# Linear attention by halves of 64 tokens in the last two of four sequences

## The chip, the cores and the metric

The program runs on one core of a Trainium2 chip. Its engines are TensorE (PE in the profile, with PEld for its weight loads), VectorE (DVE), ScalarE (ACT), GpSimd (POOL) and SyncE (SP, which issues most DMAs). The metric is the device time of one execution in microseconds, 890.63 us as the median of three runs (887.6 to 891.57).

## The reference

Four sequences of 576 tokens go through causal attention without a softmax (8 heads of 64, with a decay per head), and then through two feed-forward layers of 512 to 2048 to 512:

```python
ret = scores * Dmat          # scores = q k^T / sqrt(64); Dmat = gamma**(i-j) for i >= j, else 0
x = np.matmul(ret, v)        # per head; heads side by side make 2304 tokens x 512
h = x @ w_in;  g = np.where(h > 0, h, np.exp(np.minimum(h, 0)) - 1);  x = g @ w_out
h = np.maximum(x @ w_in2, 0);  out = (h * h) @ w_out2
```

## The kernel before

The decay is taken into q and k beforehand (`scale_chunk`, L261: one multiplication each on DVE, or on POOL for the first block). Attention then runs by chunks of up to 128 tokens, each in three pieces (`attn_pieces`, L271):

- `transposes` (L288): q and k to heads-by-tokens on PE, two heads to a group of 128 partitions, and copied out by ACT into `qT` and `kT`.
- `scores` (L300): per head K·Qᵀ, masked by DVE (L309) into `P0` (even heads) and `P1` (odd heads; `P1` takes the place of `kT`).
- `values` (L315): what earlier tokens give is read from the state `st` (L321), what the chunk itself gives is P·V (L325), both into one PSUM bank, which is split into a high and a low float32r part (`split`, L157: ACT, then DVE). Then KᵀV of the chunk (L335) is added to `st` by DVE (L341).

Attention is in plain float32: each such matmul of the program leaves two records in the trace, each with its own weight load. `st` is block-diagonal: of each 128x128 block, two heads' 64x64 squares are filled. PSUM for attention is a pool of two banks (`ps_a`, L142) through which all its tiles rotate; q, k and v have two buffers each (`n_p`, L137).

The tokens lie in five blocks (`BLOCKS`, L24; 512, 512, 256, 512, 512). The first layer is done unit by unit (`up`, L353, twelve matmuls of 128x128 weights; `down`, L374, twelve more, two units later), and the pieces of attention for the next block stand between ACT's and DVE's part of a unit (`mid`, L798), by `SPREAD` (L41). A chunk's loads are issued after the chunk two before it is done (`load_next`, L716). The first two sequences' chunks lie in the first block, the second and the first half of the third; the chunks of the last two sequences are done during the units of the second, third and fourth block. A scheduler then sets the order on each engine by its own estimate of times, and each engine works in that order; PE's matmuls of the layers and of attention stand between one another.

Of the kernel before, what the change touches and what calls it, by code (L numbers as in the profile page):

```python
# [9 lines left out]
F32 = mybir.dt.float32  # L10
# [4 lines left out]
ALU = mybir.AluOpType  # L15

B, H, S, D = 4, 8, 576, 64
NT, DM, DFF = B * S, H * D, 2048
P = 128
NP = H // 2  # L20
KC = DM // P
NF = DFF // P
TB = 512
BLOCKS = [(0, 512), (512, 512), (1024, 256), (1280, 512), (1792, 512)]  # L24
NB = len(BLOCKS)
LAG = 2
WARM = 3

AHEAD = 2
# [32 lines left out]
CW = COLS // NCH  # L62
NU = COLS // P
COL0 = [t // 2 for t, _ in BLOCKS]
# [8 lines left out]
def tokens(half, u):  # L73

    blk = max(b for b in range(NB) if COL0[b] <= u * P)
    t, n = BLOCKS[blk]
    return t + half * n // 2 + u * P - COL0[blk]

# [1 line left out]

MOST = float(np.array([0x7F7FF000 >> 3], np.uint32).view(np.float32)[0])

C_ID, C_MASK, C_S = 0, 128, 256


def chunks_of_blocks():
# [3 lines left out]
    for t, n in BLOCKS:  # L90
        end, cs = t + n, []
        while t < end:
            b, s = divmod(t, S)
            n = min(P, S - s, end - t)
            cs.append((b, s, n))
# [9 lines left out]
def scale_cols(s):  # L105
    c = C_S + 2 * H * STARTS.index(s)
    return c, c + H


def constants():  # L110


    c = np.zeros((P, C_ALL), np.float64)
    i = np.arange(P)
    gamma = 1.0 - 2.0 ** (-5.0 - np.arange(H))
    c[:, C_ID:C_ID + P] = np.eye(P)
    c[:, C_MASK:C_MASK + P] = i[:, None] <= i[None, :]
    for s in STARTS:
        e = (s + i - S // 2)[:, None].astype(np.float64)
        cq, ck = scale_cols(s)  # L120
        c[:, cq:cq + H] = gamma[None, :] ** e / np.sqrt(D)
        c[:, ck:ck + H] = gamma[None, :] ** -e
    return c.astype(np.float32)
# [3 lines left out]
def tile_kernel(ctx: ExitStack, tc, q, k, v, w_in1, w_out1, w_in2, w_out2, cst, out):  # L127
    nc = tc.nc
    pool = lambda name, bufs, **kw: ctx.enter_context(tc.tile_pool(name=name, bufs=bufs, **kw))
    const = pool("const", 1)  # L130
# [19 lines left out]

    wo2s = dram.tile([7 * HF, P, 2, DM // 2], F32, tag="wo2s", name="wo2s")
    cs = const.tile([P, C_ALL], F32, name="cs")
    st = const.tile([P, NP, P], F32, name="st")
    ident, mask = cs[:, C_ID:C_ID + P], cs[:, C_MASK:C_MASK + P]


    def split(pair_hi, pair_lo, src, eng=nc.vector):  # L157

        nc.scalar.copy(pair_hi, src)  # L159
        eng.tensor_tensor(out=pair_lo, in0=src, in1=pair_hi.bitcast(F32), op=ALU.subtract)  # L160
# [56 lines left out]
    def fetch_w(u, spare=None):  # L217
        a = a_p.tile([P, NP, P], F32, tag=spare, name="f") if spare else f_p.tile([P, DM], F32, tag="f", name="f")
        if spare:
            a = a.rearrange("s a b -> s (a b)")  # L220
        nc.sync.dma_start(out=a, in_=w2s[u[1] * NF + u[2]])
        f32s[u] = a
# [13 lines left out]
    nat, spare = {}, {}  # L236
    x_t = {}
# [23 lines left out]
    def scale_chunk(ch):  # L261
# [4 lines left out]
        for t, c in zip((qn, kn), scale_cols(ch[1])):  # L266
            eng.tensor_tensor(
                out=t[:n], in0=t[:n], in1=cs[:n, c:c + H].unsqueeze(2).to_broadcast([n, H, D]), op=ALU.mult
            )

    def attn_pieces(ch, blk):  # L271
        b, s, n = ch
        o = b * S + s - BLOCKS[blk][0]
        live = {}

        def psum(name, w=P):
            if ch in aside[::2]:
                return ps_acc.tile([P, 512], F32, tag="acc", name=name)[:, :NP * w].rearrange("s (p i) -> s p i", p=NP)
            return ps_a.tile([P, NP, w], F32, tag="a", name=name)

        def sbuf(name):
            if ch not in aside:

                return a_p.tile([P, NP, P], F32, tag="kT" if name == "P1" else name, name=name)

            return spare[ch][("P1", "k", "v", "qT", "kT", "P0").index(name)].rearrange("s (p i) -> s p i", p=NP)

        def transposes():  # L288
            qn, kn, _ = nat[ch]
            for t, nm in ((qn, "qT"), (kn, "kT")):  # L290
                ps = psum("ps_t")
                for p in range(NP):
                    nc.tensor.transpose(
                        ps[:, p, :n], t[:n, 2 * p:2 * p + 2, :].rearrange("s h d -> s (h d)"), ident[:n, :n]
                    )
                tt = sbuf(nm)
                live[nm] = tt
                nc.scalar.copy(tt[:, :, :n], ps[:, :, :n])

        def scores():  # L300
            qT, kT = live["qT"], live["kT"]
            ps = [psum("ps_s") for e in range(2)]
            for p in range(NP):
                for e in range(2):
                    r = slice(e * D, (e + 1) * D)
                    nc.tensor.matmul(ps[e][:n, p, :n], kT[r, p, :n], qT[r, p, :n], start=True, stop=True)  # L306
            for e in range(2):
                pt = sbuf(f"P{e}")
                nc.vector.tensor_tensor(  # L309
                    out=pt[:n, :, :n], in0=ps[e][:n, :, :n],  # L310
                    in1=mask[:n, :n].unsqueeze(1).to_broadcast([n, NP, n]), op=ALU.mult,
                )
                live[e] = pt

        def values():  # L315
            qT = live["qT"]
            _, kn, vn = nat[ch]
            ps = psum("ps_o")

            for p in range(NP if s else 0):  # L320
                i = nc.tensor.matmul(ps[:, p, :n], st[:, p, :], qT[:, p, :n], start=p == 0, stop=True, skip_group_check=True)  # L321
                tc.stamp_issue_order_token(i.ins, f"state{b}_{s}")
            for p in range(NP):
                for e in range(2):
                    nc.tensor.matmul(  # L325
                        ps[e * D:(e + 1) * D, p, :n], vn[:n, 2 * p + e, :], live[e][:n, p, :n],
                        start=not s, stop=True, skip_group_check=True,
                    )
            x = x_t[blk]
            split(x[:, :, 0, o:o + n], x[:, :, 1, o:o + n], ps[:, :, :n])  # L330
            if s + n < S:
                pu = psum("ps_u", D)
                for p in range(NP):
                    for e in range(2):
                        nc.tensor.matmul(  # L335
                            pu[e * D:(e + 1) * D, p, :], kn[:n, 2 * p + e, :], vn[:n, 2 * p + e, :], start=True, stop=True
                        )
                for e in range(2):
                    r = slice(e * D, (e + 1) * D)
                    if s:  # L340
                        nc.vector.tensor_tensor(out=st[r, :, r], in0=pu[r], in1=st[r, :, r], op=ALU.add)  # L341
                    else:
                        nc.vector.tensor_copy(st[r, :, r], pu[r])
            del nat[ch]

        return [transposes, scores, values]


# [356 lines left out]
    w2 = [(1, 0, f + h * HF) for f in range(HF) for h in range(2)] + [(1, 1, f + h * HF) for f in range(HF) for h in range(2)]  # L705

    nc.sync.dma_start(out=cs, in_=cst)
    nc.vector.memset(st, 0.0)

    warm = ps_h.tile([P, 512], F32, tag="h", name="warm")  # L710
    for _ in range(WARM):
        nc.tensor.matmul(warm, st[:, 0], st.rearrange("p a b -> p (a b)"), start=True, stop=True)
    at = dict(load=0, scale=0, next=0, raw=0, f32=0, split=0, raw2=0, f322=0, park=0, fetch=0, split2=0)
    todo = []

# [10 lines left out]
    def attn_step():  # L726
        if not todo and at["next"] < len(chunks):
            ch, blk = chunks[at["next"]]
            if blk not in x_t:
                new_x(blk)  # L730
            todo.extend(attn_pieces(ch, blk))
            at["next"] += 1
        if todo:
            todo.pop(0)()
            if len(todo) == 1:
                scale_next()
            if not todo:
                load_next()
# [23 lines left out]

    new_x(0)
    first = [attn_pieces(ch, 0) for ch in blocks[0]]
    load_next()
    load_next()
# [30 lines left out]
    for i, (blk, f) in enumerate(ORDER1):  # L797
# [30 lines left out]
        pend.append((blk, f))  # L828
        if len(pend) > LAG:
            down(*pend.pop(0))  # L830
# [76 lines left out]
```

## Time and profile before

| | |
|---|---|
| median of three runs | 890.63 us |
| profiled execution, span of it | 890.2 us, 888.4 us |
| busy: PE, PEld, DVE, ACT | 858.9, 773.1, 685.8, 491.9 us |
| granted TensorE clock over the span | 0.99 |

The profile is of one execution. Times in rows are microseconds from the start of the span. A PE record's end is modelled, and records of one engine overlap, so what a matmul costs is read from the distance between starts. Attention of the last two sequences lies at about 230 to 410 us, the first layer ends near 520 us.

### The profile page before, as it was taken

How to read it: one execution, taken by the hardware profiler on the slowest of the kernel's cores; microseconds unless marked ns; L12 is line 12 of the kernel's file. 1: busy time of each engine (PE TensorE's matmuls, PEld its weight loads, DVE VectorE, ACT ScalarE, POOL GpSimd, SP SyncE). 2: the span in 40 equal slices, each digit the busy share in tenths (PEclk: the TensorE clock that was granted, in tenths of full speed). 3: DMA queues.
4: the chain of work that ended last, by engine and by line, in shares of the span. 5: the costliest groups of instructions: out<-in, count | busy, mean ns of one | idle time of the engine just before them, and what ended most of it. 6: DMA issues, size and time to landing. Idle time of an engine off the chain costs nothing.

```text
span 888.4 us, 14958 instructions
## 1 busy us (share of the span) xinstructions
PE 858.9 (97%) x5630; PEld 773.1 (87%) x5630; DVE 685.8 (77%) x1391; ACT 491.9 (55%) x961; POOL 8.6 (1%) x12
## 2 busy tenths in 40 slices
PE   7798999999998999999999999999999989999998
PEld 5676888888888988888888899999989989999997
DVE  4998888885667867766779867889874769898984
ACT  3674778673464666556767754555543434444441
POOL 3000000000000000000000000000000000000000
PEclk9999899999999999999999999999999999999999
DMA  9945306383528656534362044599997993544331
GB/s 223 269 117 160 87 33 190 119 213 96 142 60 233 173 156 184 171 107 146 129 230 89 24 126 154 161 325 349 344 324 242 402 346 132 157 141 154 120 131 37
DMA packets 157608, 155.33 MB, mean 175 GB/s; under 512 B 62816, under 2 KB 121312, under 8 KB 157536
## 3 DMA queue, kind: packets, MB, share of 16 engines
q1 hardware_dynamic: 150208, 139.69, 52.0%
q10 hardware_dynamic: 7328, 14.68, 4.6%
q8 instruction: 44, 0.72, 0.4%
q14 instruction: 28, 0.23, 0.1%
HBM read 98.77 MB, written 55.57 MB: 174 GB/s over the span
## 4 chain that ended last, share of the span: by engine, by line
PE 83%; DVE 6%; DMA 5%; issue 2%; ACT 2%; SPq 1%; ACTq 0%; DVEq 0%
PE m L675 18%; PE A L492 10%; PE acc L163 7%; PE acc L164 7%; PE h L163 7%; PE acc L165 7%; PE h L164 7%; PE h L165 7%; PE D L492 5%; PE B L492 2%; PE ps_o L325 2%; PE ps_o L321 1%; PE ps_s L306 1%; DMA q<-in_q_dram 1%; DMA g<-g2s 1%
## 5 line engine op out<-in xcount | busy, mean ns | idle before, releaser
L675 PE MATMUL m<-wo,S 128*128 128x256 f32 x1512 | 184.0, 285 | 3.6 <-ACT S L159 3.6
L675 PEld LDWEIGHTS m<-wo,S 128*128 128x128 f32 x1512 | 183.3, 193 | 4.1 <-ACT S L159 4.0
L159 ACT CAST S<-g 128x512 fp32r<-128x512 f32 (+1 forms) x144 | 75.0, 567 | 95.0 <-DVE g L659 45.9
L163 PE MATMUL h<-x,w 128*128 128x512 f32 (+1 forms) x320 | 120.4, 378 | 2.2 <-DVE t L370 1.3
L164 PE MATMUL h<-x,w 128*128 128x512 f32 (+1 forms) x320 | 118.9, 372 | 0.0
L165 PE MATMUL h<-x,w 128*128 128x512 f32 (+1 forms) x320 | 118.9, 371 | 0.0
L164 PE MATMUL acc<-g,w 128*128 128x512 f32 (+1 forms) x320 | 118.5, 371 | 0.0
L165 PE MATMUL acc<-g,w 128*128 128x512 f32 (+1 forms) x320 | 117.5, 370 | 0.0
L492 PE MATMUL A<-T,pair 128*128 128x384 f32 x576 | 114.2, 339 | 1.6 <-DVE go L519 0.8
L163 PE MATMUL acc<-g,w 128*128 128x512 f32 (+1 forms) x320 | 111.4, 375 | 2.3 <-DVE x L402 1.3
L492 PEld LDWEIGHTS A<-T,pair 128*128 128x128 f32 x576 | 102.0, 190 | 3.4 <-DVE go L519 1.6
L160 DVE TENSOR_TENSOR S<-g,S 128x512 fp32r<-128x512 f32 (+1 forms) x144 | 85.9, 623 | 23.2 <-ACT S L159 21.7
L365 ACT ACTIVATE t<-h 128x512 f32<-128x512 f32 (+1 forms) x80 | 44.5, 556 | 80.5 <-PE h L165 76.9
L369 DVE SCALAR_TENSOR_TENSOR t<-e,t 128x512 f32<-128x512 f32 (+1 forms) x80 | 50.9, 636 | 46.7 <-ACT t L367 46.5
L163 PEld LDWEIGHTS h<-x,w 128*128 128x128 f32 x320 | 60.7, 190 | 14.1 <-DVE t L370 1.8
L159 ACT CAST g<-t 128x512 fp32r<-128x512 f32 (+1 forms) x80 | 46.4, 580 | 46.5 <-DVE t L370 44.7
L163 PEld LDWEIGHTS acc<-g,w 128*128 128x128 f32 x320 | 59.4, 188 | 13.4 <-DVE x L402 1.6
L165 PEld LDWEIGHTS h<-x,w 128*128 128x128 f32 x320 | 60.8, 190 | 10.7 <-DVE w L160 0.2
L164 PEld LDWEIGHTS h<-x,w 128*128 128x128 f32 x320 | 60.9, 190 | 10.2
L164 PEld LDWEIGHTS acc<-g,w 128*128 128x128 f32 x320 | 60.3, 188 | 10.2
L165 PEld LDWEIGHTS acc<-g,w 128*128 128x128 f32 x320 | 60.2, 188 | 10.1
L492 PE MATMUL D<-T,pair 128*128 128x384 f32 x288 | 58.5, 336 | 1.9 <-ACT pair L159 0.6
(88 smaller groups left out, 1282.4 us busy)
## 6 DMA issues: line engine op xcount, KB each, us to landing
g2s<-go SPq DMA_DIRECT2D x48, 384.0 KB, 4.5
g<-g2s SPq DMA_DIRECT2D x36, 512.0 KB, 3.9
raw<-in_moe_w_in_dram SPq DMA_DIRECT2D x32, 512.0 KB, 5.8
raw<-in_moe_w_out_dram SPq DMA_DIRECT2D x32, 512.0 KB, 4.8
wo2s<-wo SPq DMA_DIRECT2D x56, 256.0 KB, 4.2
wo<-wo2s ACTq DMA_DIRECT2D x9, 1536.0 KB, 14.7
w2s<-f SPq DMA_DIRECT2D x32, 256.0 KB, 2.3
f<-w2s SPq DMA_DIRECT2D x32, 256.0 KB, 4.0
```

The lines of the kernel that those rows point to most:

```text
L159: nc.scalar.copy(pair_hi, src)
L160: eng.tensor_tensor(out=pair_lo, in0=src, in1=pair_hi.bitcast(F32), op=ALU.subtract)
L163: nc.tensor.matmul(ps, l_hi, r_hi, start=first, stop=False)
L164: nc.tensor.matmul(ps, l_hi, r_lo, start=False, stop=False)
L165: nc.tensor.matmul(ps, l_lo, r_hi, start=False, stop=last)
L306: nc.tensor.matmul(ps[e][:n, p, :n], kT[r, p, :n], qT[r, p, :n], start=True, stop=True)
L321: i = nc.tensor.matmul(ps[:, p, :n], st[:, p, :], qT[:, p, :n], start=p == 0, stop=True, skip_group_check=True)
L325: nc.tensor.matmul(ps[e * D:(e + 1) * D, p, :n], vn[:n, 2 * p + e, :], live[e][:n, p, :n], start=not s, stop=True, skip_group_check=True,)
L365: nc.scalar.activation(t, h, AF.Relu, scale=-1.0)
L369: nc.vector.scalar_tensor_tensor(out=t, in0=e, scalar=1.0, in1=t, op0=ALU.add, op1=ALU.mult)
L492: ins = nc.tensor.matmul(ps, w[:, l, o:o + P], t[:, r, j], start=first and i + j == 0, stop=i + j == 3, skip_group_check=True)
L675: ins = nc.tensor.matmul(m(u, k), l[:, x], w[:, y], start=first and k in (1, 6, 4, 5), stop=j == HF - 1 and i == 2, skip_group_check=True,)
```

## The change

The first two sequences keep their code (now `scores_whole` and `values_whole`). `P0` no longer has a buffer: for chunks that don't lie in spare room it takes the place of the chunk's own q. The last two sequences go by halves of 64 tokens within a chunk. Scores are made only for the two squares on the diagonal (64 keys by 64 queries per head); the lower left square is left to the state, which now advances by 64 tokens and has two buffers, `sts`, used in turn. A half's KᵀV is made in the scores piece, in the same two PSUM banks as the scores, and added to the state from one buffer into the other; the second half's is first copied by ACT to where q was, and added at the end of `values`. Both masked halves of P lie in the place of `kT`. The values of a half are read from its own state (128 rows by 64 columns of weights, 64 tokens) and from P. The constants get a 64-column mask, and both states are cleared at the start.

```diff
-C_ID, C_MASK, C_S = 0, 128, 256
+C_ID, C_MASK, C_HALF, C_S = 0, P, 2 * P, 2 * P + HC
...
             if ch not in aside:
-
+                if name == "P0":
+                    return nat[ch][0].rearrange("s h d -> s (h d)").rearrange("s (p i) -> s p i", p=NP)
...
+        def add_state(to, st, u):
+            for (out_, r), (in_, _) in zip(spread(to), spread(st)):
+                nc.vector.tensor_tensor(out=out_, in0=u[r], in1=in_, op=ALU.add)
...
         def scores():
+            qT, kT = live["qT"], live["kT"]
+            _, kn, vn = nat[ch]
+            banks = [psum("ps_s").rearrange("s p i -> s (p i)") for _ in range(2)]
+            part = lambda i, r: banks[i][:, r * NP * HC:(r + 1) * NP * HC].rearrange("s (p i) -> s p i", p=NP)
+            for p in range(NP):
+                for e in range(2):
+                    for h in halves:
+                        nc.tensor.matmul(
+                            part(e, 0)[hs[h], p, :], kT[hs[e], p, hs[h]], qT[hs[e], p, hs[h]], start=True, stop=True
+                        )
+            kept = [h for h in halves if s + (h + 1) * HC < S]
+            for p in range(NP):
+                for h in kept:
+                    for e in range(2):
+                        nc.tensor.matmul(
+                            part(h, 1)[hs[e], p, :], kn[hs[h], 2 * p + e, :], vn[hs[h], 2 * p + e, :], start=True, stop=True
+                        )
+            pt = sbuf("kT").rearrange("s p (e i) -> s e p i", e=2)
+            live["P"] = pt
+            for e in range(2):
+                nc.vector.tensor_tensor(
+                    out=pt[:n, e], in0=part(e, 0)[:n], in1=mask[:n].unsqueeze(1).to_broadcast([n, NP, HC]), op=ALU.mult
+                )
+            for h in kept:
...
+                if not at_:
+                    for out_, r in spread(to):
+                        nc.scalar.copy(out_, u[r])
+                elif h and s:
+                    live["u"] = nat[ch][0].rearrange("s h d -> s (h d)")[:, :NP * HC].rearrange("s (p i) -> s p i", p=NP)
+                    nc.scalar.copy(live["u"], u)
+                else:
+                    add_state(to, state[b, at_], u)
+
+        def values():
...
+            ps = [psum("ps_o", HC) for _ in halves]
+            reads = [h for h in halves if s + h * HC]
+            order = [("r", h, e, p) for h in reads for p in range(NP) for e in range(2)]
+            order += [("v", h, e, p) for p in range(NP) for h in halves for e in range(2)]
+            for i, (kind, h, e, p) in enumerate(order):
+                out_ = ps[h][hs[e], p, :]
...
+                        out_, state[b, s + h * HC][:, p, hs[e]], qT[:, p, hs[h]], start=p == 0, stop=True,
...
+                        out_, vn[hs[h], 2 * p + e, :], pt[hs[h], e, p, :], start=not s + h * HC, stop=True,
...
+            for h in halves:
+                c = slice(o + h * HC, o + (h + 1) * HC)
+                split(x[:, :, 0, c], x[:, :, 1, c], ps[h])
+            if "u" in live:
+                add_state(state[b, s + n], state[b, s + HC], live["u"])
+            del nat[ch]
...
+        if b < WHOLE:
+            return [transposes, scores_whole, values_whole]
         return [transposes, scores, values]
...
-    nc.vector.memset(st, 0.0)
+    for st in sts:
+        nc.vector.memset(st, 0.0)
```

The change also gives the scheduler another order to make. On PE, at the values of the fourth sequence's chunk from token 192 on, it stood before as follows; `ps_o` is the values' PSUM bank, `ps_u` that of KᵀV, `acc` and `h` belong to the feed-forward layer.

```order
L165 MATMUL acc_3473<-g,w_706 128x512
L321 MATMUL ps_o<-qT,st 128x128 x4
L325 MATMUL ps_o<-P_3653,v 64x128
L325 MATMUL ps_o<-P_3655,v 64x128
L325 MATMUL ps_o<-P_3653,v 64x128
L325 MATMUL ps_o<-P_3655,v 64x128
L325 MATMUL ps_o<-P_3653,v 64x128
L325 MATMUL ps_o<-P_3655,v 64x128
L325 MATMUL ps_o<-P_3653,v 64x128
L325 MATMUL ps_o<-P_3655,v 64x128
L335 MATMUL ps_u<-v,k 64x64 x8
L163 MATMUL acc_3474<-g,w_706 128x512
```

After the change the same chunk has two places on PE, its scores with both halves' KᵀV (L326, L333) and, some units' matmuls later, its values (L369 reads of the two states, L374 P·V):

```order
L165 MATMUL acc_3649<-g,w_436 128x512
L326 MATMUL ps_s<-qT,kT 64x64 x16
L333 MATMUL ps_s<-v,k 64x64 x16
L166 MATMUL acc_3649<-g,w_436 128x512
...
L165 MATMUL acc_3649<-g,w_704 128x512
L369 MATMUL ps_o<-qT,st_110 64x64 x8
L369 MATMUL ps_o<-qT,st_109 64x64 x8
L374 MATMUL ps_o<-kT,v 64x64 x16
L166 MATMUL acc_3649<-g,w_704 128x512
```

KᵀV moved from the end of the values to the end of the scores, and four matmuls of 128 columns became sixteen of 64. In the third sequence DVE's order moves too. Before, after the last sum of the second block (`x`, L402) the masks of the chunk from token 256 on (L309, into `P`) stood ahead of the scaling of the next chunk's q (L267):

```order
L402 TENSOR_TENSOR x_2420<-acc_2188,x_2420 128x512
L369 SCALAR_TENSOR_TENSOR t<-e,t 128x256
L309 TENSOR_TENSOR P_2624<-ps_s,cs 128x512
L309 TENSOR_TENSOR P_2626<-ps_s,cs 128x512
L370 TENSOR_TENSOR t<-h,t 128x256
L206 TENSOR_SCALAR f<-f 128x512
L207 TENSOR_SCALAR f<-f 128x512
L208 SCALAR_TENSOR_TENSOR f<-raw,f 128x512
L160 TENSOR_TENSOR g<-t,g 128x256 x2
L211 ISA f<-raw,f 128x1024
L267 TENSOR_TENSOR q<-q,cs 128x512
L160 TENSOR_TENSOR x<-ps_o,x 128x4x128
```

Now the scaling of that next chunk's q (L269) stands ahead of the same chunk's masks (L339, into `kT`) and of the addition to the state (L301):

```order
L213 ISA f<-raw,f 128x1024
L162 TENSOR_TENSOR g<-t,g 128x256
L269 TENSOR_TENSOR q<-q,cs 128x512
L339 TENSOR_TENSOR kT<-ps_s,cs 128x4x64
L301 TENSOR_TENSOR st_110<-ps_s,st_109 64x4x64 x2
L339 TENSOR_TENSOR kT<-ps_s,cs 128x4x64
L269 TENSOR_TENSOR k<-k,cs 128x512
```

The masks have moved behind an instruction that needs a load of the next chunk. On PE that chunk's values have moved too: before, four `acc`, three `h` and twelve `acc` matmuls of 256 columns and then the next unit's twelve `h` stood behind them; now these stand ahead of them, with two more of `acc`.

## Rows read from the trace of the kernel before

**Rows 1.** The page's first part: busy time and share of each engine
```profile
PE 858.9 (97%) x5630; PEld 773.1 (87%) x5630; DVE 685.8 (77%) x1391; ACT 491.9 (55%) x961; POOL 8.6 (1%) x12
```

**Rows 2.** Busy time by stretch (windows), with instructions, granted clock and DMA share
```profile
243.00:320.00 77.00, 73.80 (x702) 68.65 (x701) 58.03 (x126) 42.95 (x100) 0.00 (x0) 1.00 0.58 155
320.00:410.00 90.00, 89.70 (x555) 74.17 (x554) 65.61 (x120) 55.92 (x100) 0.00 (x0) 1.00 0.52 153
```

**Rows 3.** PE's waits, 243 to 410 us: releaser, us in total, times, longest
```profile
PE acc L163 <- DVE x L402: 1.3, 1, 1.3
PE ps_t L293 <- DVE x L160: 1.2, 1, 1.2
```

**Rows 4.** Timeline of PE at the values of a middle chunk: start, length
```profile
334.16 0.39 PE L165 MATMUL h<-x,w 128*128 128x512 f32 x1
334.38 1.05 PE L321 MATMUL ps_o<-qT,st 128*128 128x128 f32 x8
335.37 1.09 PE L325 MATMUL ps_o<-P,v 128*64 128x128 f32 x16
336.29 0.63 PE L335 MATMUL ps_u<-v,k 128*64 128x64 f32 x16
336.86 0.50 PE L163 MATMUL h<-x,w 128*128 128x512 f32 x1
337.19 0.40 PE L164 MATMUL h<-x,w 128*128 128x512 f32 x1
```

**Rows 5.** The same view at the scores of the last chunk
```profile
399.14 0.39 PE L165 MATMUL h<-x,w 128*128 128x512 f32 x1
399.37 0.39 PE L163 MATMUL acc<-g,w 128*128 128x512 f32 x1
399.69 1.16 PE L306 MATMUL ps_s<-qT,kT 64*128 64x128 f32 x16
400.78 0.50 PE L164 MATMUL acc<-g,w 128*128 128x512 f32 x1
401.12 0.39 PE L165 MATMUL acc<-g,w 128*128 128x512 f32 x1
```

**Rows 6.** The same view at two 64-token chunks between 256-column matmuls
```profile
305.86 1.00 PE L321 MATMUL ps_o<-qT,st 128*128 128x64 f32 x8
...
317.66 0.28 PE L164 MATMUL acc<-g,w 128*128 128x256 f32 x1
317.78 0.28 PE L165 MATMUL acc<-g,w 128*128 128x256 f32 x1
317.99 0.68 PE L325 MATMUL ps_o<-P,v 64*64 64x64 f32 x16
318.51 0.63 PE L335 MATMUL ps_u<-v,k 64*64 64x64 f32 x16
319.07 0.74 PE L163 MATMUL acc<-g,w 128*128 128x256 f32 x4
```

**Rows 7.** Line 335 there: length of a record, shortest, median, longest, in ns
```profile
L335 PE MATMUL ps_u<-v,k x16: 218/218/218, 318.5 to 318.9; 64*64 64x64 f32 x16
```

**Rows 8.** Line 306 in 20 ns: busy us, records that run, clock
```profile
330.16:330.18 0.02, 0.01 (x2) 1.00 0.00 0
```

**Rows 9.** DVE by line and shape, the whole span: busy us, mean ns
```profile
L309 DVE TENSOR_TENSOR P<-ps_s,cs 128x512 f32<-128x512 f32 x26 | 17.0, 686 | 11.7 <-PE ps_s L306 11.6
L160 DVE TENSOR_TENSOR x<-ps_o,x 128x256 fp32r<-128x256 f32 x4 | 1.7, 422 | 1.8 <-ACT x L159 1.8
```

**Rows 10.** Timeline of SP's issues near 275 us
```profile
270.71 4.91 SPq L411 DMA_DIRECT2D x2s<-x  x8
275.73 0.38 SPq L256 DMA_DIRECT2D q<-in_q_dram  x1
```

**Rows 11.** Timeline of DVE near 279 us
```profile
279.05 0.69 DVE L267 TENSOR_TENSOR q<-q,cs 128x512 f32<-128x512 f32 x1 [2.51 <-DMA q<-in_q_dram]
```

**Rows 12.** Timeline of PE there: first matmul of the next unit
```profile
278.09 0.28 PE L163 MATMUL h<-x,w 128*128 128x256 f32 x1
```

## What was predicted

> **What bounds the kernel now.** I read the page's first part, then busy time by stretch, PE's waits, PE's timeline at one chunk of each kind, and DVE and SP where the order changes. PE is busy for 97% of the span [rows 1]. What bounds it here is read from the stretches in which the changed chunks lie: PE works 73.8 of 77 us and 89.7 of 90 us, at a granted clock of 1.00, while DVE works 58.0 and 65.6 us and ACT 43.0 and 55.9 us [rows 2]. PE's two longest waits there come to 2.5 us, both on DVE's `x` [rows 3]. So a microsecond of PE work saved is a microsecond of the end, as long as DVE's order doesn't keep PE waiting.
>
> What PE spends on a chunk is read from starts, not lengths. Between matmuls of the layers (512 columns, one start each .22 to .23 us), the values of a chunk of 128 take from 334.38 to 336.86, and the first layer matmul behind them needs .33 instead of .23: 2.48 + .10 = 2.58 us, of which KᵀV (L335) is .57 [rows 4]. A chunk's scores take from 399.69 to 400.78, with .32 instead of .23 in front and .34 instead of .23 behind: 1.09 + .09 + .11 = 1.29 us [rows 5]. Together a chunk costs PE 3.87 us, without its transposes, which stay.
>
> **The price of a 64x64 matmul.** Each float32 matmul leaves two records. L335's 16 records take .63 us from first start to last end and one lasts .218, so they came in 8 steps of (.63 − .218)/7 = .058 us, two records each [rows 6, 7]: the two half-wide tiles work at once. The pair's starts lie within .02 us [rows 8]. A visit to small tiles between layer matmuls has a price of its own: L325 and L335 there are 32 records, 16 steps, .93 us, but take 317.99 to 319.07 = 1.08, which leaves .15 for filling, emptying and the change of shape [rows 6]; with .09 ahead [rows 5] and .10 on the first layer matmul behind [rows 4] a visit costs .34 us.
>
> After the change a middle chunk has scores of 32 records on four tiles (two halves of keys by two heads), KᵀV of 32 on four tiles, reads of 32 on two tiles (they use all 128 rows of a state), and P·V of 32 on four. The trace shows no four tiles at once. If all four work as two do, a step holds four records: 8 + 8 + 16 + 8 = 40 steps of .058 = 2.32 us. From above, a set of four could cost as much as two pairs, .116, which makes 64 steps = 3.71 us; nothing in the rows says that four could be quicker than the one step. I take the first: in a pair the second tile costs nothing beside the first [rows 8], L335 of a whole chunk fills and uses the whole array as two tiles of 128 rows in the same .058 (.63 us for 16 records [rows 4]), so that four quarters ask no more of it, and, by the code, the two row halves write to different banks (`banks[e]` by head for scores, `banks[h]` and `ps[h]` by half for KᵀV and values). The Trainium skill, TensorEngine Tiling (Array Packing), section Restrictions and Gotchas, says that different row tiles can't write to one bank at the same time; the change keeps to it, so by that rule four run at once and the sum is the one taken, and no row here shows four.
>
> **The sum on PE.** 40 steps 2.32, two visits (scores with KᵀV; values) .68, and the change from reads to P·V inside a visit .15: 3.15 to 3.17 us, against 3.87. That saves .70 per middle chunk. There are six such chunks in the two sequences: 4.2 us. The third sequence's first chunk had no reads before (3.87 − .99, and .09 for entering = 2.97) and now has them for one half (3.17 − .46 = 2.71): .26. The 64-token chunks have one half, so only two tiles, and scores, KᵀV and P·V cost the same: nothing at the fourth sequence's first; at the third's last the reads, eight records of the full array at (1.00 − .22)/7 = .111 [rows 6], .89, become 8 steps of .058, less .15 for the change of shape: .27. The fourth's last chunk had no KᵀV (3.87 − .57) and now has one for its first half, on two tiles (3.17): .13. In all 4.9 us. Against it: the new order on PE returns 35 times from small tiles to a layer matmul where it was 33, because some pieces are cut by a layer's matmul; 2 × .34 = .68. Net 4.2 us.
>
> **DVE and ACT.** A middle chunk's masks were two of 128x512 at .686, the split one of the same length, and the sum into the state two of 128x256 length at .42: 2.9 us. Now masks, splits, and sums are eight of that shorter length, 8 × .42 = 3.36: .46 more [rows 9]. ACT gets the copy of the second KᵀV, about as much, .5. Ten chunks give some 4 us on each at most. It is hidden by DVE's 19 and 24 idle us and ACT's 34 each in the two stretches [rows 2]; without that cover it is 4 us. The second cleared state and the 64 more columns of constants lie at the start, before the first data; I bound them between 0 and .5 us (DVE's length for 128x512 is .686, for which it has nothing else to do) and take 0. `P0`'s lost buffer and the second state cost no time. But q's place is free later, since it now holds `P0` or the KᵀV, and the next-but-one chunk's q load goes behind it on SP, with k, v and raw weights behind that; a chunk ahead is still loaded, so I take 0, and put the other end under the second rival. One more chance lies below nothing: PE's waits of 1.3 and 1.2 us [rows 3] can go when DVE's order moves.
>
> The profiled execution took 890.2 us, 1.8 more than its span and 0.4 less than the median. 890.2 − 4.2 = 886.0 against its own; from the median, 890.6 − 4.2 = **886.4 us**. Its own range is 882.5 (both waits gone as well, rounded up) to 889 (the net saving cut to 1.6 by the DVE and ACT additions of which a part isn't hidden).
>
> **Rivals.**
>
> *Four tiles cost as much as two pairs.* Then 736 records of scores (256), KᵀV (224) and P·V (256) cost .029 each rather than .0145: 10.7 us more, so 886.4 + 10.7 = 897.1, slower than before. For it: no row shows more than two at once, and four tiles want twice as many instructions in a step as two. Against it: second tiles came free. It decides as soon as a set of four takes over about .082, where the saving of 4.2 is eaten up (4.2 us over 184 sets = .023 over .058). A weaker form from the Trainium skill, TensorE: Matmul & The Clock Gate, section "Wait — 56ns, not 53.3ns?", is that starts never come closer than about 25 ns: an estimate by it is 736 × (.025 − .0145) = 7.7 us, so 894.1. The trace has starts closer than that inside a pair [rows 8], though on average one per .029, so it speaks against the rule in its strict form and can't rule it out as a mean.
>
> *A load stands before the masks.* In the third sequence DVE now scales the next chunk's q before it masks the scores of (2, 256). Before, this q's load is issued at 275.73, behind eight stores of `x2s` [rows 10], and DVE could scale it at 279.05 after 2.51 us idle [rows 11]. If the load comes no earlier, the state for the chunk's second half is there at 279.05 + .69 + .42 + .84 = 281.0 (scale, one mask, two sums). PE, by the old times, reaches those reads when the next unit's twelve `h` and two `acc` matmuls are done: 278.09 + 14 × .12 = 279.8 [rows 12], minus the values of 2.6 that used to lie ahead = 277.2, and .5 later for the second half's reads, 277.7. It waits about 3.3 us, and 886.4 + 3.3 = 889.7: no change. For it: the order is fixed and the stores on SP are the same. Against it: SP's stores can start earlier, as PE's work ahead is shorter, and PE lost 1.2 us at this spot already, waiting for DVE's `x` [rows 3].
>
> *The waits of 1.3 and 1.2 us go.* 886.4 − 2.5 = 883.9. For it: the DVE order changes at both spots; against it, something has to come in their place.
>
> **How the numbers follow.** Main case .54, of which faster .24, same .29, slower .01: 886.4 lies on the border itself, since what a measurement of this kernel can tell from no change is about 0.5%, 4.45 us, so 886.2. Four as two pairs .16 (slower .14, same .02). Load before the masks .17 (same .16, slower .01). Waits gone .13, faster. Sum: faster .37, same .47, slower .16. The range 882.5 to 893 leaves out the first rival nearly whole and a little below.
>
> **What would show it.** Right: L326 and L333 of a middle chunk start to start in about .94 us, with four records' starts inside the first 25 ns of a set; values of .93 (L369) and .47 (L374); layer matmuls still .23 apart; granted clock 1.00 at 243 to 410 us; PE's busy time about 4 us lower. Wrong: L326 with 32 records in .93 instead of .47 (pairs); a wait of PE at L369 or L374 for DVE's `kT` or `st` near 278 to 281 us, or DVE idle ahead of the scaling of q there (the load); or PE's busy time 4 us lower and the end not, with new waits on DVE elsewhere.

## The result: slower by 1.4%, and where the time lies in the profile after

The changed kernel takes 901.4 us (median of five runs, 898.5 to 903.1), the kernel before 888.4 us in its five runs: ratio 1.0138, interval 1.0104 to 1.0172. The forecast was 886.4 us in a range of 882.5 to 893. The profiled execution has a span of 899.9 us against 888.4 us, 11.5 us more.

The page's first part, after:

```profile
PE 862.2 (96%) x6206; PEld 770.9 (86%) x6206; DVE 686.5 (76%) x1412; ACT 494.4 (55%) x979; POOL 9.2 (1%) x12
```

PE was to lose 4 us of busy time and has gained 3.3 [rows 1]. The same stretches as in [rows 2] (busy time of PE, PEld, DVE, ACT, POOL; granted clock; DMA share; GB/s):

```profile
243.00:320.00 77.00, 69.55 (x854) 63.09 (x854) 51.79 (x119) 41.06 (x98) 0.00 (x0) 0.98 0.60 161
320.00:410.00 90.00, 88.54 (x839) 72.65 (x838) 68.44 (x136) 55.93 (x110) 0.00 (x0) 1.00 0.53 153
```

PE now stands still for 7.5 us of the first stretch, where it stood for 3.2, and the clock is no longer full there. But what the forecast's sum rests on is as it said. PE's timeline at a middle chunk that no layer matmul cuts, its scores with KᵀV (L326, L333) and its values (L369, L374):

```profile
364.05 0.39 PE L165 MATMUL acc<-g,w 128*128 128x512 f32 x1
364.37 0.69 PE L326 MATMUL ps_s<-qT,kT 64*64 64x64 f32 x32
364.88 0.65 PE L333 MATMUL ps_s<-v,k 64*64 64x64 f32 x32
365.46 0.50 PE L166 MATMUL acc<-g,w 128*128 128x512 f32 x1
365.80 0.39 PE L167 MATMUL acc<-g,w 128*128 128x512 f32 x1
...
370.81 0.39 PE L165 MATMUL acc<-g,w 128*128 128x512 f32 x1
371.13 1.15 PE L369 MATMUL ps_o<-qT,st 128*64 128x64 f32 x32
372.21 0.69 PE L374 MATMUL ps_o<-kT,v 64*64 64x64 f32 x32
372.83 0.50 PE L166 MATMUL acc<-g,w 128*128 128x512 f32 x1
373.17 0.40 PE L167 MATMUL acc<-g,w 128*128 128x512 f32 x1
```

32 records of scores start within .51 us, where pairs would need .93. In their first 20 ns four records run (L326 alone: busy us, records, clock, DMA share, GB/s):

```profile
364.37:364.39 0.02, 0.02 (x4) 1.00 0.00 0
```

The first visit costs 1.09 + .09 + .11 = 1.29 us, the second 1.70 + .09 + .11 = 1.90: 3.19 us, forecast 3.15 to 3.17, before 3.87 [rows 4, 5]. So the saving is there, and something else takes 16 us (11.5 and the 4.2 forecast).

How far PE has come tells where. The layer's 1920 matmuls (`h` and `acc`) are the same in all kernels here; the table gives the start of the 151st (before any half is computed) and of the last one, in us of the span.

| kernel | 151st | last | span |
|---|---|---|---|
| before | 98.8 | 518.4 | 888.4 |
| changed | 104.6 | 529.3 | 899.9 |
| e1 all whole | 104.6 | 526.6 | 896.9 |
| e2 P0 at q alone | 100.9 | 522.5 | 892.3 |
| e3 halves in one sequence | 103.6 | 525.3 | 896.9 |
| e4 scaling later | 104.7 | 523.9 | 891.8 |
| e5 wide constants alone | 102.7 | 520.9 | 889.6 |
| e6 mask apart | 100.2 | 522.8 | 892.5 |
| e7 and P0 in the second state | 99.1 | 519.4 | 887.9 |
| e8 and scaling later | 99.3 | 519.7 | 887.6 |
| e9 and first scores in one piece | 99.3 | 517.6 | 887.0 |
| e10 pairs | 99.8 | 525.4 | 895.2 |

5.8 us are gone before 105 us, in the first two sequences, whose steps are the old ones, with `P0` in another place. Another 5.1 come between 200 and 410 us, on balance, after the halves' saving. The largest single place is the third sequence's first chunk: from the 701st to the 801st matmul (237 to 265 us) the lag behind the kernel before grows from 5.4 to 10.4 us. DVE's timeline (start, length, what it waited for):

```profile
242.54 0.75 DVE L339 TENSOR_TENSOR kT<-ps_s,cs 128x256 f32<-128x256 f32 x2
243.39 0.88 DVE L301 TENSOR_TENSOR st<-ps_s,st 64x256 f32<-64x256 f32 x2
247.57 0.69 DVE L269 TENSOR_TENSOR q<-q,cs 128x512 f32<-128x512 f32 x1 [3.30 <-DMA q<-in_q_dram]
252.79 0.69 DVE L269 TENSOR_TENSOR k<-k,cs 128x512 f32<-128x512 f32 x1 [4.53 <-DMA k<-in_k_dram]
253.40 0.69 DVE L459 SCALAR_TENSOR_TENSOR t<-e,t 128x512 f32<-128x512 f32 x1
```

DVE stands 7.8 us at the next chunk's q and k, and the unit's own work (`t`) is queued behind them. In the kernel before it stood there too, for k alone, and PE's wait on `t` was .5 us:

```profile
243.20 0.69 DVE L267 TENSOR_TENSOR k<-k,cs 128x512 f32<-128x512 f32 x1 [4.10 <-DMA k<-in_k_dram]
```

SP's issues say why the loads are late: they stand behind sixteen stores of `x2s`, and k behind two raw weights as well. In the kernel before the same stores stand ahead of q, but earlier: they begin at 226.47, and q goes out at 234.00.

```profile
235.45 8.93 SPq L501 DMA_DIRECT2D x2s<-x  x16
244.43 0.43 SPq L258 DMA_DIRECT2D q<-in_q_dram  x1
244.91 1.18 SPq L189 DMA_DIRECT2D raw<-in_moe_w_in_dram  x2
246.13 0.50 SPq L258 DMA_DIRECT2D k<-in_k_dram  x1
```

PE runs out of work and then works at half clock. Its timeline, and below it busy time and granted clock by 2 us:

```profile
252.71 0.28 PE L165 MATMUL h<-x,w 128*128 128x256 f32 x1
254.87 0.39 PE L165 MATMUL h<-x,w 128*128 128x256 f32 x1 [1.88 <-DVE t L460]
...
256.13 0.41 PE L165 MATMUL h<-x,w 128*128 128x256 f32 x1
256.35 0.41 PE L166 MATMUL h<-x,w 128*128 128x256 f32 x1
```

```profile
252.00:254.00 2.00, 0.98 (x5) 1.00 0.15 27
254.00:256.00 2.00, 1.13 (x7) 0.92 0.00 0
256.00:258.00 2.00, 2.00 (x11) 0.50 0.03 8
258.00:260.00 2.00, 2.00 (x15) 0.73 0.00 0
```

A 256-column matmul starts each .21 to .22 us there instead of .12 [rows 6]; .50 is 1.2 GHz. The clock costs 2 x (.08 + .50 + .27) = 1.7 us besides the 1.88. PE's two longest waits from 225 to 410 us (us in total, times, longest) are on `t`, where the kernel before had .7 us, and on the sums `x`, where it had 1.3; its wait of 1.2 us on the split `x` is down to .2:

```profile
PE h L165 <- DVE t L460: 5.1, 5, 1.9
PE acc L165 <- DVE x L492: 3.0, 3, 1.6
```

At (2, 256), the place of the prediction's second rival, DVE stood 2.0 us before the next chunk's q, which it scaled at 287.73, and PE then waited for the state:

```profile
289.67 1.46 PE L369 MATMUL ps_o<-qT,st 128*64 128x64 f32 x32 [0.73 <-DVE st L301]
```

### The profile page after: what moved, and what is told of

The parts are those of the page before. It is cut to its first block, busy times and chain, and to the rows that moved or that the text cites. A ratio compares the mean times of both kernels' runs of the same rounds, so it can differ in the third digit from the quotient of the medians.

```text
span 899.9 us, 16159 instructions
## 1 busy us (share of the span) xinstructions
PE 862.2 (96%) x6206; PEld 770.9 (86%) x6206; DVE 686.5 (76%) x1412; ACT 494.4 (55%) x979; POOL 9.2 (1%) x12
## 4 chain that ended last, share of the span: by engine, by line
PE 71%; DVE 11%; DMA 10%; ACT 3%; SPq 2%; issue 2%; ACTq 1%; DVEq 0%
PE m L765 18%; PE A L582 8%; PE h L165 6%; PE acc L165 6%; PE h L166 6%; PE h L167 6%; PE acc L166 6%; PE acc L167 6%; PE D L582 4%; PE B L582 2%; DMA k<-in_k_dram 2%; DMA part<-parts 1%; DMA g<-g2s 1%; SPq L258 1%; DMA q<-in_q_dram 1%
## 5 line engine op out<-in xcount | busy, mean ns | idle before, releaser
L165 PEld LDWEIGHTS h<-x,w 128*128 128x128 f32 x320 | 61.4, 193 | 18.9 <-DVE t L460 7.7
L167 PEld LDWEIGHTS h<-x,w 128*128 128x128 f32 x320 | 61.5, 192 | 10.7 <-DVE w L162 0.2
L166 PEld LDWEIGHTS h<-x,w 128*128 128x128 f32 x320 | 61.5, 192 | 10.2 <-DVE x L162 0.2
```

The lines of the kernel that those rows point to most:

```text
L165: nc.tensor.matmul(ps, l_hi, r_hi, start=first, stop=False)
L166: nc.tensor.matmul(ps, l_hi, r_lo, start=False, stop=False)
L167: nc.tensor.matmul(ps, l_lo, r_hi, start=False, stop=last)
```

## Experiments

Theory A: the halves save on PE what was forecast; the first two sequences lose time by what the change does to them on the side; and DVE's waits for loads eat the saving. Rivals: the halves cost it all (B), P0's place costs everywhere (C). Each ratio is to the kernel before on the same chip, with its 95% interval, five rounds each; e1 to e4, e5 to e8, and e9 with e10 ran on three different chips.

**e1, all four sequences whole.**

```diff
-WHOLE = 2
+WHOLE = 4
```

> The changed kernel with all four sequences by whole chunks; P0 in the place of q, the second cleared state and the wider constants stay. Theory A (the 5.8 us that the changed kernel has lost by 99 us come from what the change does to the first two sequences, most of it P0 in the place of q, and the other 5 us are lost in the third sequence, where DVE stands before a load): 888.4 + 5.8 = 894.2, ratio 1.0065, the loss there before 100 us. Rival B (it is the halves that cost it all, the start differs by chance from run to run): 888.4, ratio 1.000. Rival C (P0 in the place of q also delays loads later on, and the halves give their 4 us): 901.4 + 4 = 905, ratio 1.019.

Measured: 899.0 us, 1.0123 (1.0101 to 1.0146), and 104.6 us at the 151st matmul, as in the changed kernel. Nearly the whole loss is there without a half being computed. B falls, and C's 1.019 isn't reached. The loss is twice what A allotted to this part (in the profile 5.8 us of it by the 151st matmul and 8.2 at the last, with `P0` in the place of q in all four sequences); the halves make 1.0138 out of 1.0123, no difference within the intervals. From the 601st matmul to the last, this kernel and the changed one have the same chunks to do. By starts, attention apart from the transposes takes 31.9 us here and 26.6 there: 5.4 us saved, where 4.9 were forecast. But PE's idle time rises from 4.4 to 9.7 us, and the layer's matmuls by 2.5, of which the half clock shown above is 1.7; here the granted clock is 1.00 over that part.

**e2, P0 in the place of q, alone, in the kernel before.**

```diff
             if ch not in aside:
+                if name == "P0":
+                    return nat[ch][0].rearrange("s h d -> s (h d)").rearrange("s (p i) -> s p i", p=NP)
                 return a_p.tile(...)
```

> The kernel before with one part of the change alone: P0 in the place of q in the chunks that are not in spare room. Theory A: the start loses 5.8 us as in the changed kernel, 894.2, ratio 1.0065. Rival (the second state's clearing, the wider constants or chance make the start longer): 888.4, ratio 1.000.

Measured: 895.1 us, 1.0070 (1.0045 to 1.0096). So P0's place costs some 6 us by itself, of which the profile has 2.1 by the 151st matmul and 4.1 at the last. The ratio is near A's 1.0065, but not for A's reason: the start was to lose 5.8 us alone. SP's issues of the first two of three q loads of the second sequence, before and then in e2:

```profile
38.34 0.67 SPq L256 DMA_DIRECT2D q<-in_q_dram  x1
46.79 1.62 SPq L256 DMA_DIRECT2D q<-in_q_dram  x1
```

```profile
45.18 0.37 SPq L256 DMA_DIRECT2D q<-in_q_dram  x1
60.26 0.37 SPq L256 DMA_DIRECT2D q<-in_q_dram  x1
```

They come 6.8 and 13.5 us later, the third 8.3 (74.08 instead of 65.79). SP's longest waits for such loads, before and then in e2 (up to 110 us, total, times, longest):

```profile
SPq L256 <- PE ps_u L335: 18.2, 2, 11.2
```

```profile
SPq L256 <- DVE q L310: 22.6, 3, 9.2
```

L310 is the mask that writes P0, there named q. It had ended 2.3 to 4.5 us before these loads; what they follow is the values' last read of P0, at the load of 60.26 this one of PE:

```profile
59.96 0.27 PE L326 MATMUL ps_o<-q,v 128*64 128x128 f32 x1
```

A buffer that was free after the transposes is now free after the values, SP stops at its load, and raw weights queue behind (47.16 and 62.05 instead of 45.77 and 60.74). PE's wait of `acc` for split weights goes from .8 to 2.0 us. The written order moves too: PE returns from attention to the layer 62 times up to the last matmul, where it was 56.

**e3, halves in the fourth sequence alone.** `WHOLE = 3`.

> The changed kernel with halves in the fourth sequence alone, the third by whole chunks. Theory A: the 5.8 us of the start stay, the third sequence loses nothing, the fourth saves its share of the PE work, about 2.4 us: 888.4 + 5.8 - 2.4 = 891.8, ratio 1.004. Rival B (halves cost in each sequence alike): 888.4 + 5.8 + 2.5 = 896.7, ratio 1.009.

Measured: 900.5 us, 1.0131 (1.0103 to 1.0158). More than either expected, as in e1, because the loss without halves was taken too low (5.8 instead of the 10.9 that e1's ratio gives). Against e1 it is no difference: in the fourth sequence alone the halves bring nothing on balance. The 2.4 us expected of them lie at the edge of what the two intervals can tell apart, but the profiles agree: from the 601st matmul to the last it is 313.9 us here and 314.1 in e1.

**e4, the next chunk's q and k scaled a unit later.** In the last two sequences only, behind that later unit's elementwise work on DVE:

```diff
+DELAY = 0
...
             if len(todo) == 1:
-                scale_next()
+                if chunks[at["next"] - 1][0][0] >= WHOLE:
+                    late.append(2)
+                else:
+                    scale_next()
...
         up(blk, f, mid)
+        for j, left in enumerate(late):
+            late[j] -= 1
+        while late and late[0] <= DELAY:
+            late.pop(0)
+            with tc.issue_after(last_of(mybir.EngineType.DVE)):
+                scale_next()
```

> The changed kernel, but in the last two sequences DVE scales the next chunk's q and k one unit later, behind that unit's own elementwise work, so that a late load no longer stops the layer. Theory A: the third sequence's 5 us come back in most part, 901.4 - 4.5 = 897, ratio 1.010, with PE's waits of 1.9 us on t and 0.7 us on st gone. Rival B (the halves themselves cost it): 901, ratio 1.014. Rival D (the wait only moves to PE's transposes, which need the scaled q): 899 to 902.

Measured: 896.1 us, 1.0082 (1.0058 to 1.0105), 5 us less than the changed kernel, as A has it. On DVE at that place the scaling no longer stands still, but its unit's `t` comes first:

```profile
246.91 0.69 DVE L460 SCALAR_TENSOR_TENSOR t<-e,t 128x512 f32<-128x512 f32 x1 [4.65 <-ACT t L458]
249.62 0.68 DVE L270 TENSOR_TENSOR q<-q,cs 128x512 f32<-128x512 f32 x1
```

PE has no wait from 225 to 265 us any more.

**e5, 64 columns of constants that nothing reads, in the kernel before.** `C_S` at 320 instead of 256.

> The kernel before with 64 more columns of constants that nothing reads (464 instead of 400), loaded first as before; nothing else. Theory A2 (the wider first load moves the written order of the start: the scores of the 64-token chunk go from behind 2 to behind 22 matmuls of the first unit, and this costs what the changed kernel loses beyond P0's place, 5.8 - 2.1 = 3.7 us by 99 us): 888.4 + 3.7 = 892.1, ratio 1.004. Rival (the columns are a load of 32 KB, nothing else matters): 888.5, ratio 1.000.

Measured: 893.1 us, 1.0049 (1.0029 to 1.0070): 4.3 us for 32 KB that nobody reads. The bytes hold nothing up at first: the first layer matmul starts at 34.1 us, before at 36.0. What moves is the written order: the scores of the first sequence's 64-token chunk stand 20 layer matmuls further back. That the scheduler does this because it takes the first load to be longer is inferred, as its estimates were not looked at. PE at that chunk, before and then in e5 (in brackets the idle time and its cause):

```profile
36.70 0.68 PE L306 MATMUL ps_s<-qT,kT 64*64 64x64 f32 x16
42.45 1.00 PE L321 MATMUL ps_o<-qT,st 128*128 128x64 f32 x8
```

```profile
41.07 0.68 PE L306 MATMUL ps_s<-qT,kT 64*64 64x64 f32 x16
45.07 1.11 PE L321 MATMUL ps_o<-qT,st 128*128 128x64 f32 x8 [2.65 <-DVE P L309]
```

The scores come 4.4 us later, their masks with them, and the reads wait 2.65 us where they waited for nothing. Then the clock falls, as at 256 us above; before and then e5 by 5 us (busy time of PE, granted clock, DMA share, GB/s):

```profile
40.00:45.00 5.00, 4.64 (x40) 1.00 1.07 339
45.00:50.00 5.00, 4.82 (x23) 1.00 0.96 222
```

```profile
40.00:45.00 5.00, 2.41 (x24) 1.00 1.15 333
45.00:50.00 5.00, 4.93 (x34) 0.66 0.50 127
```

The changed kernel waits at the same place for 1.8 us.

**e6, the changed kernel with its half mask loaded apart**, as the last 64 columns, so that the first load has its old width. SP issues this second load at 26.0 us, 25 us behind the first, and not some 190 us later as the text expected of e6 has it.

> The changed kernel with its half mask as the last 64 columns, loaded by a DMA of its own some 190 us later; P0 stays in the place of q. Theory A2: the start loses 2.1 instead of 5.8 us, 901.4 - 3.7 = 897.7, ratio 1.0105. Rival (the wider load has no part in it): 901, ratio 1.014.

Measured: 897.1 us, 1.0098 (1.0064 to 1.0132); the 151st matmul comes at 100.2 instead of 104.6. As expected; by the ratio alone it can't be told from the changed kernel's 1.0138 (1.0104 to 1.0172), by the trace it can.

**e7, e6 with P0 in the second state.** The second state is free until the third sequence, so P0 of the first two lies there, and it is cleared only then:

```diff
                 if name == "P0":
-                    return nat[ch][0].rearrange(...)
+                    return sts[1]
...
-    for st in sts:
-        nc.vector.memset(st, 0.0)
+    nc.vector.memset(sts[0], 0.0)
...
             ch, blk = chunks[at["next"]]
+            if ch[:2] == (WHOLE, 0):
+                nc.vector.memset(sts[1], 0.0)
```

> The changed kernel with the half mask loaded later as in e6_q_mask, and P0 of the first two sequences in the second state, which is cleared only before the third sequence: the order of the start is then that of the kernel before. Theory A2: no loss by 99 us. If the third sequence's wait of DVE for the next chunk's loads stays, 888.4 + 5.1 = 893.5, ratio 1.006; if it came from P0's place too, the 4 us of the halves remain, 884.4, ratio 0.9955. Rival B (halves cost it): 901.

Measured: 891.0 us, 1.0029 (1.0007 to 1.0051). The first two sequences now lose nothing (99.1 at the 151st, 203.4 against 203.2 at the 601st). The ratio lies between the two values expected. At the third sequence's first chunk DVE's 7.8 us before q and k are down to 1.1, though the code asks for the scaling at the same point as in the changed kernel:

```profile
238.07 0.69 DVE L270 TENSOR_TENSOR q<-q,cs 128x512 f32<-128x512 f32 x1 [0.95 <-DMA q<-in_q_dram]
239.68 0.69 DVE L270 TENSOR_TENSOR k<-k,cs 128x512 f32<-128x512 f32 x1 [0.19 <-DMA k<-in_k_dram]
```

In e6, with `P0` still in the place of q, they are 7.3. So this wait too came for the most part from where the first two sequences keep `P0`, or from the earlier clearing of the second state, which e7 changes as well. From the 601st matmul on attention is down by 3.2 us against the kernel before, but PE's idle time is up by 2.3 and the layer's matmuls by 2.0, so that nothing of the saving is left.

**e8, e7 with e4's later scaling.**

> e7_place_mask with the scaling of the next chunk's q and k one unit later as in e4_late. Theory A2: no loss at the start, no wait at the loads, the halves' saving left: 888.4 - 4 = 884.4, ratio 0.9955; bounds 881 (what e4_late gains by itself comes on top of what e7_place_mask has) and 888.5 (a new wait eats it).

Measured: 890.1 us, 1.0014 (.9995 to 1.0033). No loss, and no gain: the upper bound. Against e7 the later scaling brings nothing that the intervals show; the wait that it removed in e4 is for the most part gone in e7 already. From the 601st matmul on, attention takes 29.4 us instead of 33.5, 4.1 saved. Against that stand 2.6 us more idle time and 1.5 us on layer matmuls behind attention (45 returns instead of 41): the scheduler had cut the third sequence's first scores and KᵀV into six pieces (the text expected of e9 says seven).

**e9, e8 with that piece in one.** `tc.keep_in_program_order` on the scores and KᵀV matmuls of that chunk.

> e8_place_mask_late, in which the first scores piece of the third sequence (scores and KV products) is kept in one piece on PE instead of being cut in seven by the layer's matmuls: 6 of the layer's returns from attention fewer over the program (52 instead of 58 in the order). At the .34 us that a return costs: 6 x .34 = 2 us, from e8's 1.0014 to ratio 0.999, and to 0.998 if DVE's masks come earlier by it and the waits of 2.6 us there shrink. Rival: returns cost nothing beside the waits, ratio 1.0014 as e8.

Measured: 889.3 us, .9994 (.9971 to 1.0016): level with the kernel before. In the profile the part from the 601st matmul on is 313.9 us, 2.1 less than e8 and 1.3 less than before, with 39 returns. The intervals of e8 and e9 overlap, so that by the clock alone the 2 us are not shown. Attention is down by 5.0 us against the kernel before, and 3.7 of it go elsewhere: 2.1 to idle time, .9 to the layer's matmuls, .6 to the transposes. PE's longest waits now (from 225 to 410 us: us in total, times, longest):

```profile
PE acc L167 <- DVE x L498: 2.4, 2, 1.3
PE h L167 <- DVE t L466: 1.5, 4, 0.5
PE ps_t L310 <- DVE x L164: 0.9, 2, 0.6
```

All three are on DVE: 4.8 us, where the three on DVE before came to 3.2 (1.3, 1.2 and .7).

**e10, e9 with pairs.** The same matmuls, the first half's all before the second half's.

```diff
-            for p in range(NP):
-                for e in range(2):
-                    for h in halves:
+            for h in halves:
+                for p in range(NP):
+                    for e in range(2):
```

(and the same for KᵀV and P·V.)

> e9_tied with the halves' matmuls in another order: all of the first half's scores, KV products and P times V, then all of the second half's, so that neighbours are two tiles and never four. The same instructions. If four tiles run at once in e9_tied and only then: 184 sets of four become two sets of two, 184 x .058 = 10.7 us more, ratio 1.011. Rival (PE reorders or four at once brings nothing): ratio as e9_tied.

Measured: 893.9 us, 1.0053 (1.0029 to 1.0076), 5 us more than e9. PE at a scores piece:

```profile
360.13 0.80 PE L328 MATMUL ps_s<-qT,kT 64*64 64x64 f32 x26
...
360.94 0.92 PE L337 MATMUL ps_s<-v,k 64*64 64x64 f32 x29
361.79 0.50 PE L168 MATMUL acc<-g,w 128*128 128x512 f32 x1
```

From first score to the layer it takes 1.66 us, where the order by fours takes 1.09. So four tiles do run at once and order decides it. From the 601st matmul on attention takes 35.0 us in the profile instead of 28.5: 6.5 of the 10.7 us showed, and by the clock about half. The second half's tiles begin before the first half's are through (records of both lines lie among one another there), which fits the smaller cost.

## Why the prediction was wrong, step by step

- **The price of a 64x64 matmul, four at once: right.** 3.19 us per middle chunk against 3.17, shown in the trace and by e10. The first rival (four as two pairs) falls, and with it the weak form, a floor of 25 ns between starts: 32 records in .51 us are 16 ns each. By that rule of the Trainium skill (TensorE: Matmul & The Clock Gate, section "Wait — 56ns, not 53.3ns?") the step would be .100 us for four, as an estimate. The trace has .058 to .064, so the rule doesn't hold across tiles.
- **The sum on PE, 4.2 us: right in its main part.** e1 against the changed kernel gives 5.4 us of attention saved, where 4.9 were forecast. The .68 for two more returns didn't come: from the 601st matmul on there are 41 in the changed kernel, 43 in e1 and 41 before.
- **"The second cleared state and the 64 more columns of constants ... I bound them between 0 and .5 us ... and take 0": failed.** The columns alone cost 4.3 us (e5). I priced the DMA and the clearing as work on an engine; what they changed was the written order of a stretch of which I compared nothing. The clearing was not run alone; `P0`'s place and the columns alone (1.0070 and 1.0049) already make up e1's 1.0123 within the intervals.
- **"`P0`'s lost buffer ... cost no time. But q's place is free later ... I take 0": failed.** 6.2 us (e2, which has it in all four sequences). That the load comes later was seen; its price was put only under a rival in the third sequence, though the first two sequences, at 34 to 100 us, are where PE isn't covered.
- **"Hidden by DVE's 19 and 24 idle us": half wrong.** DVE's added .46 us per chunk is not what showed; where its instructions stand did. The second rival had the mechanism (a load stands before DVE's work). At its own place, (2, 256), it came as told, but small: PE waited .7 us instead of 3.3. The dear place is the third sequence's first chunk, where it stops the layer and not the masks, and its price is 5 us (e4). Nor does it belong to the halves: e7 has them and 1.1 us of this wait on DVE, e6 with `P0` in the place of q 7.3.
- **"PE's waits of 1.3 and 1.2 us can go": failed for the larger.** The wait on the sums `x` grew to 3.0 us in the changed kernel and 2.4 in e9; the one on the split `x` shrank to .2 and .9.
- **The range** was made of rivals that all lie in the last two sequences. 10.9 of the 12 us (e1's ratio) come without any half, and no rival had them. From the other side, e7 keeps the halves, changes only `P0`'s place, the mask's load and the clearing, and has 1.0029 instead of 1.0138.

That the cost of the wide load is one of order and not of the bytes is what e5's trace speaks for. How much of P0's place is the late loads and how much the six returns is not separated, and how the late loads and the order of the start lead to the wait in the third sequence wasn't followed further. That e9's remaining waits would go with less work on DVE was not tried.

## What to carry to other kernels

Where a scheduler writes the order by its own estimates, a change has no "untouched" part: compare the order from the first row on, also where the code is the same, and look for a piece that moved behind others just where its engine has no cover. Giving a tile the place of an input makes the input's load wait for the tile's last reader, and everything queued behind that load waits too: look for a place that is idle for the whole time (here the second state). And when work is saved on the bounding engine, find first which wait ends last once it is gone.

## What the runs showed of the hardware that was not expected

Four 64x64 tiles of float32 work in the time of one pair (32 records in .51 us, the four of a set within 20 ns), if neighbours in the order lie on different tiles; by halves the same 64 records took 1.66 us instead of 1.09 between the layer's matmuls, still less than pairs without overlap would. And a short stop can cost twice: after 1.88 us of standing still and two stretches of 2 us that were about half busy, PE was at 1.2 GHz for some 3 us, which cost about as much again (1.7 us).
